# Loading w2 in fourteen parts instead of two in a transformer block on one core

## The chip, the cores and the metric

The kernel runs on one core of a Trainium2 chip. The metric is the time of one launch on the device in microseconds (us), less is better. The engines are called as in the profile: PE (TensorE; PEld is its weight loads), ACT (ScalarE), DVE (VectorE), POOL (GpSimd) and SP (SyncE, which here only asks for DMA transfers).

## The reference

One pre-norm transformer block over 2048 rows of width 1024, all in bf16: 32 attention heads of width 32, softmax over all 2048 keys, then an MLP of width 3584 with the tanh form of gelu.

```python
x = A_x                                             # [1, 2048, 1024]
h = x + A_ref(layernorm(x), A_wqkv, A_wo)           # attention with softmax, output projection
h2 = h + B_ref(layernorm(h), B_w1, B_b1, B_w2, B_b2)

def B_ref(x, w1, b1, w2, b2):                       # w1 [1024, 3584], w2 [3584, 1024]
    h = gelu(x @ w1 + b1)
    return h @ w2 + b2
```

## The kernel before

**Stages.** The rows are cut into four chunks of 512 (`CH`, numbers 0 to 3). At the start x is loaded, normalized and turned, and keys, values and the first queries are made. Then attention runs over chunk after chunk: for each chunk, head group and half of the chunk, steps of QK^T on PE (`qk`, L1132), exp on ACT (L1141, tiles `PT`), and the product with V and with ones on PE (`pv`, L1217). While chunk n is in attention, PE does the MLP of chunk n-1 in between; the output projection and the norms belong to that, and for chunks 0 and 1 the queries of chunk n+2. The last chunk's MLP comes after all attention, in `tail`.

**Who sets the order.** A planner written in Python (`Plan`) runs while the kernel is built. It keeps an estimate of when each engine is free and when each buffer is ready, and writes every instruction into the list of its engine in the order in which it decides on it. The generators (`ffn`, `rows_out`, `tail`) hand it MLP work in small pieces: at each `yield Need(...)` the planner may put attention work first. So the order on each engine is fixed when the kernel is built; on the chip each engine goes through its list, and semaphores hold it where an operand isn't there.

**SP's list.** All transfers of the kernel are asked for by SP, in the order in which the planner recorded them. A transfer waits, on SP, for the last readers of the memory that it overwrites, and for the transfer that used its lane before: weights go round through six lanes (`lanes_w`, L274), each with a semaphore of its own, so the seventh weight transfer waits until the first has landed. What stands behind a waiting transfer in SP's list waits too.

**The MLP of a chunk (`ffn`, L1425).** The up stage makes 28 groups (`fc`, 128 of the 3584 columns each): 8 matmuls of 512 rows with w1. w1 comes in 14 pieces of 512 KB in two buffers (`loader`, L1379): piece `bk + 1` is asked for at the second group of piece `bk`. PE's matmuls here are cut into four of 32 columns (`wide`, L529), so one of them stands as four in the profile. DVE adds the bias (L1494), then DVE and ACT make the gelu (L1506 to L1509, tanh on ACT), into `gT`.

The down stage takes w2 in four quarters of 256 output columns, `q` = 0 to 3. A quarter is 3584 x 256 values, 1792 KB, 28 blocks of 128 rows. For each quarter `rows_out` runs twice (`t` = 0 and 2), each time over two tiles of 128 rows with 28 blocks: 112 matmuls of 256 columns for a quarter, and 4 for the bias. DVE adds the residual (L1412) into `ost`, and a transfer stores 128 KB; behind every second quarter's store, in chunks 0 and 1, two loads of 128 KB fetch rows of x for the next chunk (`hch`).

**Where w2 lies and when it is asked for.** Quarters 0 and 2 lie at `w2_off`, quarters 1 and 3 at `hn_off`, where the turned rows `hnT` and part of w1's buffers were in the up stage. `load_w2` (L1389) asks for a quarter as two halves of 896 KB, each with one buffer mark, so PE's first matmul of a half waits for the whole half. Quarter 0 is asked for at group 22 of the up stage (L1490), quarter 1 after the up stage (L1516), quarters 2 and 3 when quarters 0 and 1 have been recorded (L1521), as their places come free then. In `tail` quarters 0 and 1 are asked for at its beginning, and 2 and 3 as in `ffn`, at other addresses.

Of the kernel before, what the change touches and what calls it, by code (L numbers as in the profile page):

```python
# [7 lines left out]
dt = mybir.dt  # L8
# [5 lines left out]
P = 128  # L14
# [221 lines left out]
def build_kernel(nc, A_x, A_wqkv, A_wo, B_w1, B_b1, B_w2, B_b2, out):  # L236
    _, S, D = A_x.shape
# [6 lines left out]
    FC = F // P  # L244
# [29 lines left out]
    lanes_w = lanes("dw", 6)  # L274
# [5 lines left out]
    def dma(out_ap, in_ap, nbytes, reads=(), writes=(), lanes=None, noncontig=False, is_out=False, eng=E.SP):  # L280
        flow, token = lanes.next()
        if is_out and flow not in out_flows:
            out_flows.append(flow)

        def fn(s):
            if noncontig:
                with nc.allow_non_contiguous_dma(reason="strided gather"):
                    return s.dma_start(out_ap, in_ap)
            return s.dma_start(out_ap, in_ap)

        plan.task(eng, fn, reads=reads, writes=list(writes) + [token], flow=flow, nbytes=nbytes)
# [29 lines left out]
    def sb(name, shape, dtype, bufs=None, at=None):  # L321
        nbytes = mybir.dt.size(dtype)
        for d_ in shape[1:]:
            nbytes *= d_
        off = cursor[0] if at is None else at
        h = nc.alloc_sbuf_tensor_at(name, shape, dtype, offset=off)
        if at is None:
            cursor[0] = off + (nbytes + 63) // 64 * 64
        if bufs is None:
            bufs = [Buf()]  # L330
        plan.track(off, off + nbytes, bufs)
        return h, bufs

    def nbufs(n):
        return [Buf() for _ in range(n)]
# [8 lines left out]
    biasm, _ = sb("biasm", [P, G, NCH], dt.float32)  # L344
# [35 lines left out]
    v_off = cursor[0]  # L380
# [25 lines left out]
    B_ps = nbufs(8)  # L406
# [851 lines left out]
    def ffn_alloc():  # L1258
        cursor[0] = region0
        f = ffn_bufs  # L1260

        def area(name, nbytes):
            f[name] = cursor[0]
            cursor[0] += nbytes

        area("g_off", FC * 1024)
        area("x3_off", 4 * 2048)
        area("hn_off", DC * 1024)
        f["w1_off"] = cursor[0]
        f["w1"], f["B_w1"] = sb("w1", [P, 2, DC, 256], dt.bfloat16, nbufs(2))  # L1270
        f["w2_off"] = cursor[0]
        f["w2"], f["B_w2"] = sb("w2", [P, 2, FC // 2, 256], dt.bfloat16, nbufs(2))
        f["NG"] = 3
        f["tm_off"] = cursor[0]
        f["tm"], f["B_tm"] = sb("tm", [P, 3, 2, 512], dt.bfloat16, nbufs(3))
        f["n12"] = [0, 0]
        assert cursor[0] <= nc.sbuf_usable_end, (cursor[0], nc.sbuf_usable_end)
# [108 lines left out]
                writes=[B_w1_[s]], lanes=lanes_w)  # L1386
        return load

    def load_w2(ci, q, at):  # L1389
        w2, B = sb(f"w2_{ci}_{q}", [P, 2, FC // 2, 256], dt.bfloat16, nbufs(2), at=at)  # L1390
        for h in range(2):
            dma(w2[:, h, :, :], B_w2[h * FC * 64:(h + 1) * FC * 64, q * 256:(q + 1) * 256].rearrange("(c p) d -> p c d", p=P), FC * P * 256,
                writes=[B[h]], lanes=lanes_w)
        return w2, B

    def rows_out(ci, q, t, w2_, gT, B_g, g_ch, ost, B_ost, hch, B_hch):
        w2, B_w2_ = w2_
        bank = fbanks.next()
        quad = tiled[0]
        for u in range(2):  # L1400
            lo = (t + u) * P
            for fc in range(FC):
                h, i = fc // (FC // 2), fc % (FC // 2)
                if fc % 2 == 0:
                    yield Need(B_g(fc) + B_g(fc + 1) + [B_w2_[h]], [B_ps[bank]] if u == 0 and fc == 0 else [],
                               [g_ch[fc + 1]] if fc + 1 in g_ch else [])
                wide(bank, u * 256, 256, gT[:, fc, lo:lo + P], w2[:, h, i, :], fc == 0, False,
                     B_g(fc) + [B_w2_[h]], [B_ps[bank]] if fc == 0 else [], False, quad)
            wide(bank, u * 256, 256, ident[:, q:q + 1].to_broadcast([P, P]), b2row[:], False, True,
                 [B_ident, B_b2row], [B_ps[bank]], True, quad)  # L1410
        o = (q * 2 + t // 2) % len(B_ost)
        dve(lambda v: v.tensor_tensor(ost[:, o, :, :], ps[:, bank, :].rearrange("p (u c) -> p u c", u=2),  # L1412
                                      hch[:, t:t + 2, q * 256:(q + 1) * 256], ALU.add),
            reads=[B_ps[bank]] + [B_hch[2 * (t + u) + q // 2] for u in range(2)], writes=[B_ost[o]], cost=690)
        r0 = CH[ci][0] + t * P

        def store():
            dma(out2[r0:r0 + 2 * P, q * 256:(q + 1) * 256].rearrange("(u p) c -> p u c", p=P), ost[:, o, :, :], 131072,
                reads=[B_ost[o]], lanes=lanes_o, is_out=True)
            if ci < NCH - 2 and q % 2:  # L1420
                for u in range(2):
                    load_rows(r0 + 512 + u * P, t + u, q // 2)
        stores.append(chain([("call", store, [B_ost[o]], [], 0)]))

    def ffn(ci):  # L1425
# [58 lines left out]
        for bk in range(FC // 2):  # L1484
            s = w1s[bk]
            for u in range(2):
                fc = bk * 2 + u
                if u == 1:
                    load_w1(bk + len(B_w1_) - 1)
                if fc == FC - 6:  # L1490
                    w2s = [load_w2(ci, 0, f["w2_off"])]

                def evac(bank, fc=fc):
                    dve(lambda v: v.tensor_scalar(gT[:, fc, 0:w], ps[:, bank, 0:w], b1f[:, fc:fc + 1], 0.5, ALU.add, ALU.mult),  # L1494
                        reads=[B_ps[bank], Bf_b1f], writes=[B_gT[fc]], cost=100 + 1.2 * w)
                    if fc % 2 == 0:
                        return
                    gs = gelu_i[0] % NG
                    gelu_i[0] += 1
                    for c_ in list(g_ch.values()):  # L1500
                        if c_.steps and c_.slot == gs:
                            flush(c_)
                    t_, x_ = tm[:, gs, :, :], gT[:, fc - 1:fc + 1, :]
                    Bt, Bx = B_tm_[gs], B_gT[fc - 1:fc + 1]
                    g_ch[fc] = chain([
                        (E.DVE, lambda v: v.tensor_tensor(t_, x_, x_, ALU.mult), Bx, [Bt], 690),  # L1506
                        (E.DVE, lambda v: v.scalar_tensor_tensor(t_, t_, GB, x_, ALU.add, ALU.mult), [Bt] + Bx, [Bt], 1220),  # L1507
                        (E.Activation, lambda a: a.activation(t_, t_, ACT.Tanh, scale=GK), [Bt], [Bt], 946),  # L1508
                        (E.DVE, lambda v: v.scalar_tensor_tensor(x_, t_, 1.0, x_, ALU.add, ALU.mult), [Bt] + Bx, Bx, 1220)])  # L1509
                    g_ch[fc].slot = gs  # L1510

                yield from group([(w1[:, s, dc, u * P:(u + 1) * P], hnT[:, dc, 0:w]) for dc in range(DC)], evac,
                                 lambda i, s=s: [B_w1_[s]] + B_hnT[:n4], n=w)
        no = 8 if ci < LAST - 1 else 4
        ost, B_ost = sb(f"ost{ci}", [P, no, 2, 256], dt.bfloat16, nbufs(no), at=x3_at)
        w2s.append(load_w2(ci, 1, f["hn_off"]))  # L1516
        for q in range(4):
            for t in range(0, n4, 2):
                yield from rows_out(ci, q, t, w2s[q], gT, lambda fc: [B_gT[fc]], g_ch, ost, B_ost, hch, B_hch)
            if q < 2:  # L1520
                w2s.append(load_w2(ci, q + 2, f["hn_off"] if q else f["w2_off"]))  # L1521
            if q == 1 and ci == LAST - 1:
                yield from last_norm(0)
        plan.track(f["w1_off"], f["w1_off"] + 8192, B_w1_)
# [5 lines left out]
    def tail():  # L1530
# [3 lines left out]
        load_w1 = loader(w1, B_w1_, [0], w1s)  # L1534
        for bk in range(6):
            load_w1(bk)
        w2s = [load_w2(LAST, q, v_off + q * 14336) for q in range(2)]
        yield from last_norm(1)
        nd = Need()
        nd.barrier = True  # L1540
# [7 lines left out]
        def part(bank, o, fc, hf, opens):  # L1548
            hn, B_hn = last["hn", hf]
            s = w1s[fc // 2]  # L1550
            for dc in range(DC):
                yield Need([B_w1_[s]] + B_hn, [B_ps[bank]] if opens and dc == 0 else [])
                wide(bank, o, 256, w1[:, s, dc, fc % 2 * P:fc % 2 * P + P], hn[:, dc, :], dc == 0, dc == DC - 1, [B_w1_[s]] + B_hn,
                     [B_ps[bank]] if dc in (0, DC - 1) else [], dc == DC - 1, False)
# [21 lines left out]
        for q in range(4):  # L1576
            for t in (0, 2):
                yield from rows_out(LAST, q, t, w2s[q], gT, lambda fc: [B_gT[2 * fc + t // 2]], {}, ost, B_ost, hch, B_hch)
            if q < 2:
                w2s.append(load_w2(LAST, q + 2, v_off + q * 14336))  # L1580

    def fill_total(ci):
        w = CH[ci][1]
# [206 lines left out]
```

## Time and profile before

| | us |
|---|---|
| three runs: median (lowest to highest) | 1184.12 (1182.95 to 1188.19) |
| the profiled execution | 1184.54 |
| its span on the core | 1182.7 |
| PE busy, of the span | 1105.1 |
| ACT busy | 1044.2 |
| DVE busy | 668.1 |

TensorE's granted clock was 0.992 in the mean. The profile also gives the span in 40 slices, where a digit is the busy share of an engine in tenths; the DMA queues with their packets; the chain of work that ended last; and, from the trace, a timeline of each engine, where a bracket says how long the engine stood idle before a row and what ended that. "Issue" there means that the profile shows nothing that the engine waited for.

The stages of chunk 0 as an example, from the timelines of PE and SP: its up stage runs from 374 to 466 us, its four quarters begin at about 466, 490, 516 and 541 us, each some 25 us with the attention work that lies in between.

| transfers, as the page lists them | KB each | median us from issue to landing |
|---|---|---|
| w2 halves, 32 | 896 | 8.0 |
| w1 pieces in `ffn`, 42 | 512 | 3.8 |
| stores of `ost`, 24 | 128 | 3.3 |
| rows of x for `hch`, 24 | 128 | 2.7 |

### The profile page before, as it was taken

What the parts mean: (1) busy time and instruction counts of PE and PEld (TensorE: products, weight loads), DVE (VectorE), ACT (ScalarE), POOL (GpSimd) and SP (SyncE); (2) the same over time, 40 slices, a digit from 0 to 9 for tenths busy, and PEclk for the clock granted to TensorE, in tenths of its full rate; (3) what the DMA queues carried; (4) which work ended last, traced back from release to release, by engine and by line L of the source; (5) the groups of instructions that cost most, each with busy time, mean ns of one, the idle gap of its engine ahead of it and who ended that gap; (6) DMA issues with size and microseconds to landing.
All of it is one profiled execution on the core that took longest, in us unless ns stands there. A gap on an engine that the chain in (4) does not pass through costs nothing.

```text
span 1182.7 us, 54817 instructions
## 1 busy us (share of the span) xinstructions
PE 1105.1 (93%) x25609; PEld 669.0 (57%) x25614; DVE 668.1 (56%) x1178; ACT 1044.2 (88%) x1155; POOL 21.2 (2%) x60
## 2 busy tenths in 40 slices
PE   6999999999998999999999999899999999999998
PEld 3646455554444444667444445667444456577887
DVE  8564555555655788344666877444668854543001
ACT  7798999899999999999999999989999999992400
POOL 2100000000000000000000000000000000000000
PEclk9999999999999999999999999999999999999999
DMA  8301000003401236230502253330033532208523
GB/s 232 81 21 39 21 3 12 12 9 95 100 12 56 74 89 164 76 97 22 149 12 75 75 151 84 88 83 22 19 108 91 140 84 75 70 17 225 154 78 85
DMA packets 177614, 91.62 MB, mean 77 GB/s; under 512 B 39653, under 2 KB 174825, under 8 KB 177385
## 3 DMA queue, kind: packets, MB, share of 16 engines
q1 hardware_dynamic: 177384, 88.10, 27.8%
q8 instruction: 200, 3.28, 1.1%
q14 instruction: 30, 0.24, 0.1%
HBM read 83.90 MB, written 4.19 MB: 74 GB/s over the span
## 4 chain that ended last, share of the span: by engine, by line
ACT 43%; PE 42%; issue 9%; DVE 6%; DMA 0%; POOL 0%; ACTq 0%; DVEq 0%; POOLq 0%
ACT PT L1141 39%; PE ps L529 18%; PE ps L524 9%; PE ps L1217 7%; PE ps L1132 6%; ACT tm L1508 3%; DVE lnst L481 1%; PE ps L803 1%; DVE Rg L1230 1%; DVE Rg L1228 1%; DVE QT L1232 1%; PE ps L858 1%; DVE gT L1494 0%; DVE rcp L1229 0%; DVE gT L1509 0%
## 5 line engine op out<-in xcount | busy, mean ns | idle before, releaser
L1141 ACT ACTIVATE PT<-ps 128x1024 bf16<-128x1024 f32 x1024 | 953.5, 1122 | 30.0 <-PE ps L1132 19.2
L1166 DVE TENSOR_TENSOR FS<-PT 128x1024 bf16<-128x1024 bf16 x245 | 167.7, 688 | 157.7 <-ACT PT L1141 111.7
L1217 PE MATMUL ps<-PT,V 128*32 128x256 bf16 x4096 | 226.2, 274 | 18.7 <-ACT PT L1141 10.6
L1132 PE MATMUL ps<-QT,KT 32*128 32x256 bf16 x4096 | 204.7, 274 | 20.6 <-ACT PT L1141 16.7
L529 PE MATMUL ps<-w,gT 128*32 128x256 bf16 x5376 | 178.3, 275 | 7.8 <-issue 7.1
L529 PE MATMUL ps<-hnT,w 128*32 128x512 bf16 x2688 | 173.0, 381 | 6.0 <-DVE gT L1494 4.0
L1132 PEld LDWEIGHTS ps<-QT,KT 32*128 32x128 bf16 x4096 | 60.9, 92 | 170.1 <-ACT PT L1141 152.1
L529 PEld LDWEIGHTS ps<-w,gT 128*32 128x32 bf16 x5376 | 142.0, 98 | 19.6 <-issue 13.0
L1217 PEld LDWEIGHTS ps<-PT,V 128*32 128x32 bf16 x4096 | 105.4, 96 | 74.2 <-ACT PT L1141 21.8
L1217 PE MATMUL ps<-PT,ones 128*32 128x256 bf16 x2136 | 136.9, 273 | 0.0
L529 PEld LDWEIGHTS ps<-hnT,w 128*32 128x32 bf16 x2688 | 61.8, 96 | 76.8 <-issue 28.0
L1494 DVE TENSOR_SCALAR gT<-ps,b1f 128x512 bf16<-128x512 f32 x84 | 63.0, 750 | 53.9 <-PE ps L529 52.9
L1217 PE MATMUL ps<-FS,ones 128*32 128x256 bf16 x980 | 70.4, 277 | 0.3 <-DVE FS L1166 0.2
L1217 PEld LDWEIGHTS ps<-PT,ones 128*32 128x32 bf16 x2136 | 57.3, 97 | 10.8
L529 PE MATMUL ps<-xnTe,wk 128*32 128x512 bf16 x832 | 57.9, 402 | 4.3 <-DVE kmax L646 2.3
L1545 ACT ACTIVATE gT_t<-ps,b1f 128x512 bf16<-128x512 f32 (+1 forms) x36 | 20.5, 591 | 42.4 <-PE ps L524 42.4
L1412 DVE TENSOR_TENSOR ost_t<-ps,hch_t 128x512 bf16<-128x512 f32 x8 | 5.5, 692 | 88.0 <-PE ps L524 88.0
L1509 DVE SCALAR_TENSOR_TENSOR gT<-tm,gT 128x1024 bf16<-128x1024 bf16 x42 | 51.2, 1219 | 3.5 <-ACT tm L1508 3.1
L1507 DVE SCALAR_TENSOR_TENSOR tm<-tm,gT 128x1024 bf16<-128x1024 bf16 x42 | 51.3, 1220 | 0.7
L524 PE MATMUL ps<-w,gT_t 128*128 128x256 bf16 x448 | 50.7, 273 | 0.0
L524 PE MATMUL ps<-hn_t,w_t 128*128 128x256 bf16 x448 | 49.2, 273 | 0.9 <-DVE hn_t L1350 0.9
L1508 ACT ACTIVATE tm<-tm 128x1024 bf16<-128x1024 bf16 x42 | 50.1, 1193 | 0.0
(139 smaller groups left out, 942.4 us busy)
## 6 DMA issues: line engine op xcount, KB each, us to landing
w<-in_B_w_dram SPq DMA_DIRECT2D x32, 896.0 KB, 8.0
w<-in_B_w_dram SPq DMA_DIRECT2D x42, 512.0 KB, 3.8
w_t<-in_B_w_dram SPq DMA_DIRECT2D x14, 512.0 KB, 7.0
xr<-in_A_x_dram SPq DMA_DIRECT2D x16, 256.0 KB, 6.8
wk<-in_A_wqkv_dram SPq DMA_DIRECT2D x16, 256.0 KB, 3.0
wq<-in_A_wqkv_dram SPq DMA_DIRECT2D x16, 256.0 KB, 5.1
hch<-in_A_x_dram SPq DMA_DIRECT2D x24, 128.0 KB, 2.7
out_dram<-ost SPq DMA_DIRECT2D x24, 128.0 KB, 3.3
```

Source lines behind the costliest of these rows:

```text
L481: steps.append((E.DVE, lambda v, c=c: v.bn_stats(lnst[:, s, i, c * 6:(c + 1) * 6], x_ap[:, c * 512:(c + 1) * 512]), [B_x], [B], 690))
L524: pe(lambda p: p.matmul(ps[:, bank, lo:lo + n], lhsT, rhs, start=start, stop=stop), reads=reads, writes=writes, inc=inc, cost=mm(n))
L529: pe(lambda p, r=r: p.matmul(ps[32 * r:32 * r + 32, bank, lo:lo + n], lhsT[:, 32 * r:32 * r + 32], rhs, start=start, stop=stop, tile_posit ...
L1132: pe(lambda p, k=k, kt=kt, r=r, b=b: p.matmul(ps[:, b, k * 256:(k + 1) * 256], KT[32 * r:32 * r + 32, g, kt * P:(kt + 1) * P], QT[32 * r:3 ...
L1141: act(lambda a, safe, i=i, b=b: a.activation(PT[:, o_, 2 * i:2 * i + 2, :], ps[:, b:b + 2, :], ACT.Exp, bias=0.0 if safe else biasm[:, g, ...
L1166: dve(lambda v: v.tensor_tensor(FS[:, f_, :, :], PT[:, o_, :, 0:256], PT[:, o_, :, 256:512], ALU.add), reads=B_PT[o_], writes=[B_FS[f_]], ...
L1217: pe(lambda p, d=d, r=r, lhsT=lhsT, rhs=rhs, n=n: p.matmul(ps[32 * r:32 * r + 32, OD, d * 256:(d + 1) * 256], lhsT, rhs, start=(start and ...
L1494: dve(lambda v: v.tensor_scalar(gT[:, fc, 0:w], ps[:, bank, 0:w], b1f[:, fc:fc + 1], 0.5, ALU.add, ALU.mult), reads=[B_ps[bank], Bf_b1f], ...
L1507: (E.DVE, lambda v: v.scalar_tensor_tensor(t_, t_, GB, x_, ALU.add, ALU.mult), [Bt] + Bx, [Bt], 1220),
L1508: (E.Activation, lambda a: a.activation(t_, t_, ACT.Tanh, scale=GK), [Bt], [Bt], 946),
L1509: (E.DVE, lambda v: v.scalar_tensor_tensor(x_, t_, 1.0, x_, ALU.add, ALU.mult), [Bt] + Bx, Bx, 1220)])
L1545: act(lambda a: a.activation(gT[:, fc, lo:lo + n], ps[:, bank, o:o + n], ACT.Gelu_apprx_tanh, bias=b1f[:, fc:fc + 1], scale=1.0), reads=[B ...
```

## The change

In chunks 0 to 2 a quarter of w2 is asked for in 14 parts of 128 KB (two blocks of 128 rows each), and each part has a buffer mark of its own, so that PE waits part by part. `load_w2` only makes the list of parts. In `ffn` the parts of quarter 0 are asked for one at a time from group 14 of the up stage on, one at each group; those of quarter q+1 at every eighth block of quarter q's `rows_out` (16 places, of which 14 are used). What is left when a quarter begins is asked for at once. The tail (`whole=True`) still takes two halves, with seven buffer marks each. Places in memory and the matmuls are as before.

```diff
-    def load_w2(ci, q, at):
-        w2, B = sb(f"w2_{ci}_{q}", [P, 2, FC // 2, 256], dt.bfloat16, nbufs(2), at=at)
-        for h in range(2):
-            dma(w2[:, h, :, :], B_w2[h * FC * 64:(h + 1) * FC * 64, q * 256:(q + 1) * 256].rearrange("(c p) d -> p c d", p=P), FC * P * 256,
-                writes=[B[h]], lanes=lanes_w)
-        return w2, B
+    def load_w2(ci, q, at, whole=False):
+        w2, B = sb(f"w2_{ci}_{q}", [P, FC, 256], dt.bfloat16, nbufs(FC // 2), at=at)
+        parts = deque()
+        n = FC // 2 if whole else 2
+        for c in range(0, FC, n):
+            def part(c=c):
+                dma(w2[:, c:c + n, :], B_w2[c * P:(c + n) * P, q * 256:(q + 1) * 256].rearrange("(c p) d -> p c d", p=P), n * P * 512,
+                    writes=B[c // 2:(c + n) // 2], lanes=lanes_w)
+            parts.append(part)
+        while whole and parts:
+            parts.popleft()()
+        return w2, B, parts
...
-    def rows_out(ci, q, t, w2_, gT, B_g, g_ch, ost, B_ost, hch, B_hch):
-        w2, B_w2_ = w2_
+    def rows_out(ci, q, t, w2_, gT, B_g, g_ch, ost, B_ost, hch, B_hch, coming=None):
+        w2, B_w2_, parts = w2_
+        while parts:
+            parts.popleft()()
...
             for fc in range(FC):
-                h, i = fc // (FC // 2), fc % (FC // 2)
+                if fc % 8 == 0 and coming:
+                    coming.popleft()()
                 if fc % 2 == 0:
-                    yield Need(B_g(fc) + B_g(fc + 1) + [B_w2_[h]], [B_ps[bank]] if u == 0 and fc == 0 else [],
+                    yield Need(B_g(fc) + B_g(fc + 1) + [B_w2_[fc // 2]], [B_ps[bank]] if u == 0 and fc == 0 else [],
...
-                if fc == FC - 6:
+                if fc == FC // 2:
                     w2s = [load_w2(ci, 0, f["w2_off"])]
+                if fc >= FC // 2:
+                    w2s[0][2].popleft()()
...
-        w2s.append(load_w2(ci, 1, f["hn_off"]))
         for q in range(4):
+            if q < 3:
+                w2s.append(load_w2(ci, q + 1, f["w2_off"] if q % 2 else f["hn_off"]))
             for t in range(0, n4, 2):
-                yield from rows_out(ci, q, t, w2s[q], gT, lambda fc: [B_gT[fc]], g_ch, ost, B_ost, hch, B_hch)
-            if q < 2:
-                w2s.append(load_w2(ci, q + 2, f["hn_off"] if q else f["w2_off"]))
+                yield from rows_out(ci, q, t, w2s[q], gT, lambda fc: [B_gT[fc]], g_ch, ost, B_ost, hch, B_hch, w2s[-1][2] if q < 3 else None)
...
-        w2s = [load_w2(LAST, q, v_off + q * 14336) for q in range(2)]
+        w2s = [load_w2(LAST, q, v_off + q * 14336, True) for q in range(2)]
...
-                w2s.append(load_w2(LAST, q + 2, v_off + q * 14336))
+                w2s.append(load_w2(LAST, q + 2, v_off + q * 14336, True))
```

More of the change, by code (lines that the diff above doesn't have):

```diff
@@ L1271, in ffn_alloc @@
         f["w2_off"] = cursor[0]
-        f["w2"], f["B_w2"] = sb("w2", [P, 2, FC // 2, 256], dt.bfloat16, nbufs(2))
+        f["w2"], f["B_w2"] = sb("w2", [P, FC, 256], dt.bfloat16, nbufs(2))
         f["NG"] = 3
@@ L1402, in rows_out @@
             for fc in range(FC):
-                h, i = fc // (FC // 2), fc % (FC // 2)
+                if fc % 8 == 0 and coming:
+                    coming.popleft()()
                 if fc % 2 == 0:
-                    yield Need(B_g(fc) + B_g(fc + 1) + [B_w2_[h]], [B_ps[bank]] if u == 0 and fc == 0 else [],
+                    yield Need(B_g(fc) + B_g(fc + 1) + [B_w2_[fc // 2]], [B_ps[bank]] if u == 0 and fc == 0 else [],
                                [g_ch[fc + 1]] if fc + 1 in g_ch else [])
-                wide(bank, u * 256, 256, gT[:, fc, lo:lo + P], w2[:, h, i, :], fc == 0, False,
-                     B_g(fc) + [B_w2_[h]], [B_ps[bank]] if fc == 0 else [], False, quad)
+                wide(bank, u * 256, 256, gT[:, fc, lo:lo + P], w2[:, fc, :], fc == 0, False,
+                     B_g(fc) + [B_w2_[fc // 2]], [B_ps[bank]] if fc == 0 else [], False, quad)
             wide(bank, u * 256, 256, ident[:, q:q + 1].to_broadcast([P, P]), b2row[:], False, True,
```

## The prediction

> **What bounds the kernel now.** I read the page first, then the waits of each engine, then TensorE's (PE) and ScalarE's (ACT) timelines in steps of 20 us, then the DMA queues in narrow windows.
>
> ```profile
> PE 1105.1 (93%) x25609; PEld 669.0 (57%) x25614; DVE 668.1 (56%) x1178; ACT 1044.2 (88%) x1155; POOL 21.2 (2%) x60
> ...
> PE   6999999999998999999999999899999999999998
> ...
> ACT  7798999899999999999999999989999999992400
> ...
> ACT 43%; PE 42%; issue 9%; DVE 6%; DMA 0%; POOL 0%; ACTq 0%; DVEq 0%; POOLq 0%
> ```
>
> The reader is to see two engines that are both nearly full, and no share for DMA in the chain that ended last. From about 230 to 1067 us ACT stands in one unbroken run of exponentials and tanh: its timeline shows idle time in only a dozen places there. So time that ACT loses there is lost for good, and PE's idle time counts only where it makes ACT idle. The tail (1070 to 1183, PE busy 108.6 of 113.0) is PE alone, and its length hangs on nothing that the change touches.
>
> The change moves loads of w2, so I looked at what happens while those loads run. In 491 to 498 us, during the third quarter's load of the first chunk, the queues show:
>
> ```profile
> q1 hardware_dynamic: 3727, 1.89, 94.0%
> ```
>
> and in the page as a whole there is a queue of another kind:
>
> ```profile
> q8 instruction: 200, 3.28, 1.1%
> ```
>
> 200 packets of 16,384 bytes are PE's program: PE has 25,609 + 25,614 instructions, and 200 x 256 = 51,200. In 485 to 491 us this queue has 2 packets, in 491 to 498 us it has none, in 498 to 502 us again 2. The timelines at that place and at its fellows (PE, then ACT; the bracket is the idle time before the row and what ended it):
>
> ```profile
> 500.44 1.05 PE L529 MATMUL ps<-w,gT 128*32 128x256 bf16 x30 [2.32 <-issue]
> ...
> 522.45 0.39 PE L529 MATMUL ps<-w,gT 128*32 128x256 bf16 x6 [0.93 <-issue]
> ...
> 759.37 0.84 PE L529 MATMUL ps<-w,gT 128*32 128x256 bf16 x24 [2.20 <-issue]
> ...
> 786.05 0.41 PE L1217 MATMUL ps<-PT,V 128*32 128x256 bf16 x4 [1.96 <-issue]
> ```
> ```profile
> 501.87 3.80 ACT L1141 ACTIVATE PT<-ps 128x1024 bf16<-128x1024 f32 x4 [2.31 <-PE ps L1132]
> ...
> 523.33 7.44 ACT L1141 ACTIVATE PT<-ps 128x1024 bf16<-128x1024 f32 x8 [0.97 <-PE ps L1132]
> ...
> 760.59 4.72 ACT L1141 ACTIVATE PT<-ps 128x1024 bf16<-128x1024 f32 x5 [2.20 <-PE ps L1132]
> ...
> 789.41 6.59 ACT L1141 ACTIVATE PT<-ps 128x1024 bf16<-128x1024 f32 x7 [3.01 <-PE ps L1132]
> ```
>
> PE stands still "for nothing that the profile shows", in the midst of a row of matmuls of one tile whose operands are all there. Eight such stops lie in 370 to 1070 us: before 500.44, 522.45, 706.79, 735.44, 759.37, 786.05, 994.33 and 1019.00, of 2.32 + 0.93 + 0.69 + 0.38 + 2.20 + 1.96 + 1.28 + 1.47 = 11.2 us. Counting PE's instructions, each restart falls on the same place, 189 instructions into a block of 256, and 1.3 to 1.4 us after the end of an instruction packet. All eight follow a w2 load (SP issued pairs of 896 KB at 489.99, 515.71, 725.55, 750.30, 776.64, 984.71, 1009.38, and one between w1's loads from 699.06 on). So PE runs out of program: the fetch of its next 16 KB stands behind w2's packets. An undisturbed fetch starts when PE is some 215 instructions into its block; these start 2.5 to 4.2 us later than that, 3.3 us in the mean. What PE has in hand covers 1.3 to 2.8 us of it (lateness less stop, stop by stop), and the rest is the stop. [...]
>
> **The change part by part.** In the built programs the order of instructions on PE, ACT, DVE and POOL is the same before and after; only SP's queue and the semaphores waited for differ.
>
> *The two 896 KB loads of a quarter become 14 of 128 KB* (chunks 0 to 2, 4 quarters each; the tail keeps halves). What it removes is the long queue in front of the fetch: 1.8 MB at once, about 8 us of traffic (7.4 and 8.6 us to landing in these windows). ACT's idle time at the eight stops is 2.31 + 0.97 + 0.83 + 0.35 + 2.20 + 3.01 + 1.26 + 1.44 = 12.4 us, and ACT is what bounds there, so 12.4 us is the most that these stops can give. PE can follow: in 466 to 570 us it is busy 97.3 of 104 us, and 3.3 of its idle time are two of the stops.
>
> What a fetch still waits for behind parts isn't in the trace, so it gets two bounds. The low one is nothing: fetches that start with a 128 KB store or a pair of 128 KB hch loads in the 4 us before them (as at 481.77 and 509.37) start at the usual 200 to 260 instructions. The high one: a part waits for the part six before it on its lane (lanes_w, L274), so at most 6 x 131 KB = 786 KB stand in the queue; at 275 GB/s, the mean of 491.3 to 498 us, that is 2.9 us, against 3.3 us now. With the stops' own cover this leaves 1.4 + 1.3 + 0.2 + 0.1 + 1.6 + 1.6 + 1.5 + 0.2 = 7.9 us. Between them: SP issues a load in 0.37 us (the shortest and the median of its rows), 354 GB/s, against 275 served; over the 9 parts that it can send in a row (below) that piles up 9 x 0.131 - 3.3 x 0.275 = 0.27 MB, 1.0 us of waiting, less than the least cover of 1.3 us. That is nearest to the low row. Some fetches in these stages have less in hand (0.4 us), so I keep 1.0 us of stops: gain 12.4 - 1.0 = 11.4 us.
>
> *SP's queue.* 12 quarters x 12 more issues x 0.37 us = 53 us, on an engine that waits some 500 us for PE on this kind of load alone. In the built order q+1's parts stand as nine, the store of the running quarter's first row pair, five; the five wait behind that store for DVE's ost. In the first chunk: quarter starts at 465.5, store issued at 479.0, five parts land by 479.0 + 5 x 0.4 + 3.3 (median landing of a 128 KB store) = 484, next quarter at 490.0. Stores and hch rows stand behind at most nine parts, 3.3 us; now the store at 517.02 already takes 3.40 us to issue behind a pair. Nothing on PE waits for either within a quarter. In the up stage each w1 load keeps its place ahead of the parts; the last three w2 parts go out right behind w1's last load, three groups of 92 / 28 = 3.3 us ahead of their quarter, some 10 us, against 3.8 us in which w1's 512 KB land and 3.3 us for a part.
>
> *PE's waits.* 138 more matmul rows wait, one for each part. In today's trace the step from one such group of four matmuls to the next is 109 ns in the median with a wait that is already met and without one: nothing. Six of them need a separate semaphore instruction, 51 ns each: 0.3 us, in PE's own slack. If a part were late, everything in PE's order behind it would stand, QK^T too, and then ACT.
>
> Sum: the profiled execution took 1184.54 us (span 1182.7, 1.8 around it); 1184.5 - 11.4 = 1173.1. The median of the runs shown lies 0.4 us under that execution, so 1172.7 us.
>
> **The rivals.**
> *Parts still hold the fetch.* If the fetch waits for all that is outstanding and six parts always are, 7.9 us of stops stay: 1184.1 - 12.4 + 7.9 = 1179.6. For it: while 256 KB loads follow each other in 566 to 577 us, the fetches at 572.85 and 577.67 start late (350 and 303 instructions in). Against: those pieces are twice as large, and SP can hardly keep six parts in flight at 0.37 us each.
> *The stops have another cause, or come back elsewhere.* Then no change, 1184. Against: eight of eight on one boundary, none without a load. For: ACT idles 0.84, 0.84 and 1.05 us in load windows at 473.71, 966.95 and 969.95 away from the boundary, from the fixed order of the work alone. [...]
> *Slower: the parts land in a row and too late.* A quarter has 4 row tiles x 28 steps of w2; the last part is used first after 26 of these 112 steps, 5.8 of 25 us. It has 25 + 5.8 = 30.8 us from the first request, 2.2 us a part. If each landed only after the one before, at the 2.7 us of the 128 KB hch rows, 14 take 37.8 us, 7.0 us too late, in 9 quarters 63 us: 1184.1 - 12.4 + 63 = 1235. Against: hch_t's four 256 KB loads are issued within 1.97 us and land in 3.2 us in the median, so loads overlap; with six in flight 14 parts take 14 x 2.7 / 6 = 6.3 us. [...]
>
> **How the numbers follow.** Forecast 0.70, parts still hold the fetch 0.17, no effect 0.07, late parts 0.06. A measurement of this kernel can tell about 0.5% from no change, 5.9 us: under 1178.2 is faster. Faster has the forecast and a third of the second case: 0.76. Same has the rest of it and most of the third: 0.17. Slower: 0.07. The range: low end 1169.0, if the three idle places away from the boundary go as well (12.4 + 2.7 = 15.1 us); high end 1180, the second case. Outside stand the third and fourth, 0.13, and a little of the others.
>
> **What would show it.** In the profile after: no PE idle time put down to "issue" of over 0.5 us in 370 to 1070; ACT's idle time for PE's QK^T down from 19.2 us to under 9; instruction packets every 3.6 to 4 us through the load windows; attention's end, at 1067 now, near 1056; no PE wait for a w2 load. The steps are wrong if the stops vanish and the time stays (ACT does not bound), if stops of over 1 us remain (the parts hold the fetch), or if PE waits for w2 at the head of a quarter.

## The result, and the profile after

| | before | after |
|---|---|---|
| median (lowest to highest), us | 1184.09 (1182.95 to 1188.19) | 1170.71 (1167.78 to 1173.69) |
| the profiled execution, us | 1184.54 | 1167.78 |
| its span, us | 1182.7 | 1166.0 |
| mean granted clock of TensorE | 0.992 | 0.999 |

The ratio of the times is 0.9881 with a 95% interval of 0.9845 to 0.9917: faster by 13.4 us in the medians, by 9.8 to 18.4 us at the ends of the interval. The times go with the granted clock of the run: the change's four took 1167.78, 1169.32, 1172.10 and 1173.69 us at 0.999, 0.997, 0.993 and 0.991. Before's runs beside the experiments took 1178.56 (one run), 1180.99, 1184.68 and 1185.96 us in the mean at these four clocks, so at the same clock the two kernels lie 10.8 to 12.6 us apart. The instructions of PE, ACT, DVE and POOL, and their order, are those of before.

The page of the kernel after, in the lines that answer to those shown of before (busy times, the 40 slices, the instruction queue, and the chain that ended last):

```profile
PE 1097.2 (94%) x25609; PEld 666.4 (57%) x25614; DVE 668.2 (57%) x1178; ACT 1042.3 (89%) x1155; POOL 21.1 (2%) x60
...
PE   6999999899998999999999999999989999999998
...
ACT  7798999899999999999999999999999999992400
...
q8 instruction: 200, 3.28, 1.2%
...
PE 43%; ACT 41%; issue 8%; DVE 7%; DMA 0%; POOL 0%; ACTq 0%; DVEq 0%; POOLq 0%
```

Busy times are nearly what they were; what went is idle time. The same 200 packets bring the same program. The 8 among the nines of the ACT row at slice 27 of 40 is gone.

Where PE waited in 370 to 1070 us, before and then after (us in total, times, longest):

```profile
PE ps L529 <- issue: 7.8, 6, 2.3
...
PE ps L1217 <- issue: 2.0, 1, 2.0
```
```profile
PE ps L529 <- issue: 0.8, 1, 0.8
...
PE ps L506 <- issue: 0.3, 1, 0.3
```

With L1132's one wait of 1.5 us before, and L524's of 0.2 after, PE's time at "issue" went from 11.3 to 1.3 us. No row of this view names a DMA of w2 as the releaser: no part was late. Before had no such row either, so it isn't the marks by which PE now waits part by part that gain. ACT's waits for QK^T over the whole span (19.2 us, 15 times, before) are now:

```profile
ACT PT L1141 <- PE ps L1132: 4.5, 6, 1.1
```

The timeline of ACT after, at the places of the first two, the fourth, the fifth and sixth, and the last two of the eight stops: the rows of exponentials have no break there, and no bracket. (At the third, too, the timeline has no bracket.)

```profile
489.49 52.41 ACT L1141 ACTIVATE PT<-ps 128x1024 bf16<-128x1024 f32 x57
...
722.55 1.17 ACT L1519 ACTIVATE tm<-tm 128x1024 bf16<-128x1024 bf16 x1
723.50 16.72 ACT L1141 ACTIVATE PT<-ps 128x1024 bf16<-128x1024 f32 x18
...
744.56 56.19 ACT L1141 ACTIVATE PT<-ps 128x1024 bf16<-128x1024 f32 x61
...
989.47 58.88 ACT L1141 ACTIVATE PT<-ps 128x1024 bf16<-128x1024 f32 x64
```

In a window of 675 us ACT's busy time shows the same (after the stretch and its length: busy us and count of PE, PEld, DVE, ACT, POOL, then granted clock, DMA share, GB/s), before and then after:

```profile
370.00:1045.00 675.00, 635.76 (x16336) 368.01 (x16328) 424.45 (x667) 659.38 (x717) 6.69 (x15) 0.99 0.30 82
```
```profile
370.00:1045.00 675.00, 645.78 (x16800) 377.82 (x16796) 431.94 (x680) 672.16 (x732) 6.66 (x15) 1.00 0.29 82
```

**Where the 16.7 us between the two spans went.** I set the two timelines of ACT side by side, instruction by instruction. Up to about 216 us, before the first load of w2, after is 2.65 us ahead: the change does nothing there, and the clock differs (last section). At the places of the eight stops it gains 2.45, 1.33, 0.85, 0.56, 2.35, 3.34, 1.40 and 1.85 us, 14.1 in all. It gains some 1.5 us at 967 to 970 us, again a place where the clock differs. It loses 0.71 and 0.40 us, 1.1 in all, at two small stops that are new:

```profile
569.80 0.61 PE L529 MATMUL ps<-wo(1, 0)_97,QT 128*32 128x512 bf16 x8 [0.81 <-issue]
...
851.83 0.29 PE L506 MATMUL ps<-ident,x 128*32 128x128 bf16 x7 [0.31 <-issue]
```

2.65 + 14.1 + 1.5 - 1.1 = 17.2; the 0.5 over the 16.7 is spread in small losses. The two new stops stand, as the old ones did, 189 instructions into a block of 256, the first beside the 1 MB loads of wo. Without the two clock places the profiled pair differs by about 12.6 us. Of the 3.34 us at the sixth stop some 1 us is likely the clock's too: PE stood 1.96 us there and ACT 3.01, while at the other seven stops the two differ by 0.14 us at most, and a stretch of half clock follows that stop (last section). Attention ends at 1049.9 instead of 1066.9 us.

SP's queue at the first chunk's second quarter after, as its timeline has it (start, duration, line, transfer, count):

```profile
489.25 5.23 SPq L289 DMA_DIRECT2D w<-in_B_w_dram  x8
499.23 0.38 SPq L289 DMA_DIRECT2D out_dram<-ost  x1
...
502.09 8.73 SPq L289 DMA_DIRECT2D w<-in_B_w_dram  x6
```

For quarters 1 to 3 "one at a time" is so in the program's text only: SP takes most of a quarter's parts in a row, here eight in 5.23 us, 0.65 us a part.

### The profile page after: what moved, and what is told of

It is laid out like the page before. It is cut to its first block, busy times and chain, and to the rows that moved or that the text cites. A ratio compares the mean times of both kernels' runs of the same rounds, so it can differ in the third digit from the quotient of the medians.

```text
span 1166.0 us, 54971 instructions
## 1 busy us (share of the span) xinstructions
PE 1097.2 (94%) x25609; PEld 666.4 (57%) x25614; DVE 668.2 (57%) x1178; ACT 1042.3 (89%) x1155; POOL 21.1 (2%) x60
## 3 DMA queue, kind: packets, MB, share of 16 engines
HBM read 83.90 MB, written 4.19 MB: 76 GB/s over the span
## 4 chain that ended last, share of the span: by engine, by line
PE 43%; ACT 41%; issue 8%; DVE 7%; DMA 0%; POOL 0%; ACTq 0%; DVEq 0%; POOLq 0%
ACT PT L1141 38%; PE ps L529 18%; PE ps L524 9%; PE ps L1217 8%; PE ps L1132 6%; ACT tm L1519 2%; PE ps L803 1%; DVE Rg L1230 1%; DVE QT L1232 1%; DVE Rg L1228 1%; DVE lnst L481 1%; DVE gT L1505 1%; PE ps L858 1%; DVE rcp L1229 0%; DVE gT L1520 0%
## 5 line engine op out<-in xcount | busy, mean ns | idle before, releaser
L1217 PE MATMUL ps<-PT,V 128*32 128x256 bf16 x4096 | 225.9, 274 | 17.5 <-ACT PT L1141 11.1
L1132 PE MATMUL ps<-QT,KT 32*128 32x256 bf16 x4096 | 203.6, 273 | 19.3 <-ACT PT L1141 16.6
L529 PE MATMUL ps<-w,gT 128*32 128x256 bf16 x5376 | 174.6, 273 | 0.7 <-DVE gT L1505 0.4
L1132 PEld LDWEIGHTS ps<-QT,KT 32*128 32x128 bf16 x4096 | 60.7, 92 | 167.9 <-ACT PT L1141 155.5
L524 PE MATMUL ps<-w,gT_t 128*128 128x256 bf16 x448 | 50.7, 273 | 0.0
L524 PE MATMUL ps<-hn_t,w_t 128*128 128x256 bf16 x448 | 49.2, 273 | 0.9 <-DVE hn_t L1350 0.9
```

The costliest lines, as they stand in the source:

```text
L524: pe(lambda p: p.matmul(ps[:, bank, lo:lo + n], lhsT, rhs, start=start, stop=stop), reads=reads, writes=writes, inc=inc, cost=mm(n))
L529: pe(lambda p, r=r: p.matmul(ps[32 * r:32 * r + 32, bank, lo:lo + n], lhsT[:, 32 * r:32 * r + 32], rhs, start=start, stop=stop, tile_posit ...
L1132: pe(lambda p, k=k, kt=kt, r=r, b=b: p.matmul(ps[:, b, k * 256:(k + 1) * 256], KT[32 * r:32 * r + 32, g, kt * P:(kt + 1) * P], QT[32 * r:3 ...
L1217: pe(lambda p, d=d, r=r, lhsT=lhsT, rhs=rhs, n=n: p.matmul(ps[32 * r:32 * r + 32, OD, d * 256:(d + 1) * 256], lhsT, rhs, start=(start and ...
```

## The experiments

All of them compute with the order of PE's, ACT's and DVE's instructions that before and after share, so times differ by waits alone, but for what x7 leaves out. Diffs are against the change, x10's against before. The question left was not whether the stops come from the fetch of PE's program, but what such a fetch waits for: all that is outstanding when it is due (the queue), the whole of the transfer that is being moved, or a turn that is bounded; and whether the small size of the transfers, their spacing or the earlier start does the work.

Two quantities are worked out from the records for every fetch in the quarters' stages. *Lateness* is the start of the fetch's packet less the time at which PE passes instruction 215 of its block. *Outstanding* is what SP had asked for less what the queues had begun to move, at that time; it is given in KB of 1000 bytes, the sizes of transfers in KB of 1024.

| kernel | median (lowest to highest), us | ratio to before, with interval | stage, us | PE at "issue", us | lateness, mean / most, us |
|---|---|---|---|---|---|
| the change | 1170.71 (1167.78 to 1173.69) | 0.9881 (0.9845 to 0.9917) | 836.7 | 1.3 | 0.34 / 0.76 |
| x11_change_again | 1172.39 (1170.63 to 1172.52) | 0.9893 (0.9863 to 0.9923) | 839.1 | 1.4 | 0.52 / 1.01 |
| x1_at_once | 1174.68 (1174.17 to 1175.49) | 0.9916 (0.9887 to 0.9945) | 841.5 | 0.4 | 0.68 / 1.73 |
| x2_448k_spread | 1175.64 (1172.32 to 1176.56) | 0.9923 (0.9897 to 0.9949) | 843.7 | 5.2 | 1.82 / 2.93 |
| x3_256k_at_once | 1171.23 (1171.0 to 1174.43) | 0.9896 (0.9864 to 0.9929) | 840.6 | 2.4 | 1.07 / 1.79 |
| x4_half_1lane | 1182.09 (1178.14 to 1185.99) | 0.9977 (0.996 to 0.9993) | 852.5 | 8.6 | 1.89 / 3.36 |
| x5_one_1792k | 1183.54 (1181.2 to 1188.31) | 1.0006 (0.9979 to 1.0033) | 851.0 | 11.1 | 2.70 / 4.02 |
| x6_256k_7lanes | 1170.94 (1168.38 to 1173.08) | 0.9896 (0.984 to 0.9952) | 839.4 | 0.4 | 1.35 / 2.89 |
| x7_one_part | 1168.36 (1167.54 to 1172.0) | 0.9883 (0.9827 to 0.9939) | 837.3 | 0.3 | |
| x8_wo_wq_parts | 1168.96 (1165.66 to 1170.95) | 0.9885 (0.983 to 0.9939) | 836.5 | 0.6 | 0.51 / 0.97 |
| x9_q0_spread | 1168.87 (1166.0 to 1172.3) | 0.9872 (0.9839 to 0.9906) | 837.2 | 0.5 | 0.59 / 1.40 |
| x10_q0_early | 1182.99 (1179.91 to 1189.11) | 0.9988 (0.9966 to 1.001) | 854.3 | 9.5 | 2.59 / 4.55 |

The stage is that of the profiled execution from ACT's 214th instruction (at 212 to 216 us) to the end of attention; it is 851.0 us before. It leaves out what differs before w2's first load, but not the clock (last section). PE's "issue" is in 370 to 1070 us, 11.3 us before. Lateness here is over the fetches that had more than 180 KB outstanding ahead of them (12 to 20 for each kernel; before: 2.50 / 4.19). Each ratio is to runs of before beside which the kernel ran.

### Size or spacing: x1_at_once and x3_256k_at_once

x1 keeps the 128 KB parts and asks for all 14 at once, at the places where before asked for its halves. x3 is x1 with parts of 256 KB.

```diff
-                if fc == FC // 2:
+                if fc == FC - 6:
                     w2s = [load_w2(ci, 0, f["w2_off"])]
...
-        while whole and parts:
+        while parts:
             parts.popleft()()
```
```diff
-        n = FC // 2 if whole else 2
+        n = FC // 2 if whole else 4
```

> Quarters in 14 parts of 128 KB as after the change, but all 14 asked for at once, at the places where the two halves were asked for before (group 22, end of the up stage, end of the quarter before). Theory 'queue' (a fetch of PE's program waits for the w2 traffic that is outstanding, which six lanes and SP's 0.37 us a part keep short): no stops put down to issue over 0.5 us in the quarters, 1170 to 1174. Rival 'spacing' (it is the asking one at a time during the steps that helps): the eight stops of 11 us are back, 1183 to 1185. Rival 'grain' (a fetch gets its turn between two transfers, so the size of one transfer decides): 1170 to 1174.

> Seven parts of 256 KB, all asked for at once at the old places, six lanes: up to 1.5 MB outstanding, as SP issues 256 KB in 0.37 us. Queue: stops of 6 to 11 us, 1178 to 1184. Grain: one part is 0.95 us, less than PE has in hand: no stops, 1170 to 1173. Spacing: 1183 to 1185.

x1 has no stop beside w2 either, with all parts asked for together: the small parts do it, not their spacing. Whether they do it by their size, or by the little that is outstanding with them (some 0.4 MB at most when a fetch was due), x1 can't tell; x3 and x6 can. But it has a wait of a new kind, seen in PE's waits and in its timeline:

```profile
PE ps L529 <- DMA w<-in_B_w_dram: 4.8, 4, 1.9
```
```profile
456.06 1.91 PE L529 MATMUL ps<-hnT,w 128*32 128x512 bf16 x32 [1.61 <-DMA w<-in_B_w_dram]
```

These are matmuls of the up stage (`hnT`), and what is late is w1. SP's timeline shows why:

```profile
440.47 13.41 SPq L289 DMA_DIRECT2D w<-in_B_w_dram  x17
```

The 14 parts of quarter 0 stand in SP's list between two pieces of w1, and w1's next piece is asked for after them. So the spacing is worth something at quarter 0 only (here the 4.8 us), and not for the fetch. x1's median of 1174.68 us lies just above the 1170 to 1174 that were expected, where this wait was not thought of. In time x1 and the change aren't clearly apart (their intervals overlap), though at the same granted clock, 0.993, x1 took 1174.17 and 1174.90 us and the change with its repeat 1172.10 to 1172.52; the 4.8 us are shown by the trace.

x3's parts of 256 KB leave 2.4 us of stops, in small pieces of at most 0.8, where the size of the transfer alone was to leave none and the queue 6 to 11 us. It is as fast as the change within the intervals.

### Middle-sized transfers, and large ones one at a time: x2_448k_spread and x4_half_1lane

x2 asks at the places of the change for parts of 448 KB. x4 goes back to the halves of 896 KB, at the old places, but puts w2's loads on one lane of their own, so that the second half is asked for only when the first has landed. It has the change's 14 marks a quarter, but seven are set together when a half has landed.

```diff
-        n = FC // 2 if whole else 2
+        n = FC // 2 if whole else 7
```
```diff
+    lanes_2 = lanes("dz", 1)
...
-        n = FC // 2 if whole else 2
+        n = FC // 2 if whole else 14
...
-                    writes=B[c // 2:(c + n) // 2], lanes=lanes_w)
+                    writes=B[c // 2:(c + n) // 2], lanes=lanes_w if whole else lanes_2)
```

> The change's places, but four parts of 448 KB a quarter in place of 14 of 128 KB. Queue: nothing ties SP to PE's steps, so all four go out in about 1.5 us, 1.8 MB stand in the queue as before: stops of 8 to 12 us, 1180 to 1185. Spacing: asked for in four steps, so about 1171. Grain: one part is 448 KB / 275 GB/s = 1.7 us, hardly over what PE has in hand (1.3 to 2.8 us): stops under 2 us in all, 1171 to 1173.

> Two halves of 896 KB at the old places as before the change, but on one lane of their own, so that the second is asked for when the first has landed: at most 0.9 MB outstanding. The marks are part by part. Queue: a fetch waits for what is left of one half, up to 3.3 us, on average half of it; stops of 3 to 7 us, 1175 to 1180. Grain: the single transfer is as large as before, so stops of 9 to 12 us, 1181 to 1185. Spacing: 1183 to 1185.

x4 has at most 997 KB outstanding, against 1688 before, and still stops for 8.6 us: between what the queue was to give (3 to 7) and what the size of the transfer was to give (9 to 12), and nearer to the second. Of its fetches with over 690 KB ahead of them six waited 2.2 to 3.4 us, until 84 KB in the mean were left. Its PE also waits 3.5 us for w1, since SP is held by the lane. So to limit what is outstanding, with transfers that stay at 896 KB, hardly brings a gain: the ratio is 0.9977.

x2 limits nothing: 0.96 MB were outstanding in the mean, against 1.04 before. It stops for 5.2 us, and its median is 1175.64 us; none of the three expectations had that (8 to 12 us of stops for the queue, under 2 for the size, 1171 us for the spacing). So transfers of 448 KB bring part of the gain, with as much outstanding as before.

### Much outstanding, in small transfers, and in one large one: x6_256k_7lanes and x5_one_1792k

x6 is x3 with seven lanes for w2 alone, so that SP may ask for a whole quarter without a wait. x5 asks for a quarter in one transfer of 1792 KB at the old places.

```diff
+    lanes_2 = lanes("dz", 7)
...
-        n = FC // 2 if whole else 2
+        n = FC // 2 if whole else 4
```
```diff
-        n = FC // 2 if whole else 2
+        n = FC // 2 if whole else 28
```

> Seven parts of 256 KB at once at the old places, on seven lanes of their own, so that no part waits for another and all 1.8 MB stand in the queue within some 2.6 us. Queue (outstanding bytes decide): as before the change, lateness up to 4 us, stops of 9 to 12 us, 1181 to 1185. Theory 'transfer size decides': as with six lanes shared: lateness under 1.9 us, stops of 1 to 2 us, 1170 to 1174.

> A quarter as one transfer of 1792 KB, at the old places. So far the lateness of a fetch went with the size of the transfer: about 1.4 us at 128 KB, 1.7 at 256, 2.5 at 448, 2.2 to 4.2 at 896. Theory 'whole transfer' (a fetch waits until the transfer in progress is done on its DMA engine): lateness of 4 to 7 us, stops of 25 to 40 us in all, 1198 to 1215. Rival 'bounded turn' (an engine takes a bounded number of packets of one queue before it serves the other, and 896 KB are already past that): lateness 2.5 to 4.2 us and stops of 9 to 13 us as before the change, 1182 to 1186.

x6's DMA view in 484 to 496 us (packets, MB, share of 16 engines), and SP's row there:

```profile
q1 hardware_dynamic: 3422, 1.71, 53.9%
q8 instruction: 2, 0.03, 1.3%
```
```profile
488.26 4.58 SPq L290 DMA_DIRECT2D w<-in_B_w_dram  x7
```

SP asks for the whole quarter within 4.58 us, not the 2.6 that were expected, so never all of it is outstanding: up to 1038 KB stand ahead of a fetch. PE has no stop over 0.2 us in 370 to 1070, though one fetch was 2.89 us late, where under 1.9 was expected. With one transfer a quarter all stops of before are back. That allows a comparison at the same amount outstanding. Fetches in the quarters with 690 to 1050 KB ahead of them (three fetches that got in before the load's first packets are left out):

| size of one transfer | kernels | fetches | outstanding when due, mean | lateness, mean (range), us | outstanding at the fetch, mean |
|---|---|---|---|---|
| 1792 KB | x5 | 3 | 906 KB | 3.07 (2.82 to 3.24) | 108 KB |
| 896 KB | before, x10, x4 | 12 | 890 KB | 2.90 (2.17 to 3.78) | 113 KB |
| 448 KB | x2 | 3 | 997 KB | 2.38 (1.78 to 2.80) | 423 KB |
| 256 KB | x3, x6 | 18 | 831 KB | 1.43 (0.75 to 2.89) | 803 KB |

The last column counts also what SP asked for only after the fetch was due. Of the bytes that stood ahead of it when it was due, some 0.43 of 0.83 MB were still to come behind transfers of 256 KB, 0.27 of 1.00 behind 448 KB, and 0.05 of 0.9 at most behind the two larger sizes. So here, in transfers of 896 KB and more, the fetch waited until nearly everything ahead of it was gone, and in transfers of 256 KB it passed about half of it. The queue as the only cause falls by that. In before itself the fetch with the most ahead of it, 1688 KB in two halves, started after 2.43 us with 0.94 MB left, as much as the whole second half.

The whole transfer as the rule falls by x5: a fetch that was due with 1764 KB ahead of it, nearly all of one transfer, started after 3.31 us with some 730 KB of them left, and no fetch of x5 was later than 4.02 us, though a transfer of 1792 KB took 9.5 us from issue to landing in the median, and one of 128 KB, in the change, 3.5. What is left is a wait that grew with the size of the transfers (1.43 us in the mean at 256 KB, 2.38 at 448, 2.90 at 896, 3.07 at 1792) and was never over 4.6 us in these runs. x5's times are those expected of the bounded turn (2.70 us of lateness in the mean, 11.1 us of stops, 1183.54 us), but no run shows a bound itself, and how the DMA engines come to this wait isn't settled. The records don't say on which of the 16 DMA engines a packet ran, so it also isn't excluded that the fetch waits for a part of the engines only, whose share of the bytes was done earlier.

### The floor: x7_one_part

In chunks 0 to 2 only the first 128 KB of a quarter are loaded, and all 28 blocks of the quarter are multiplied with these two. So 13 of 14 parts of w2's traffic are left out, 20.5 of the 53.2 MB that the queues move in 370 to 1045 us.

```diff
+        parts = deque()
+        if not whole:
+            w2, B = sb(f"w2_{ci}_{q}", [P, 2, 256], dt.bfloat16, nbufs(1), at=at)
+            dma(w2[:], B_w2[0:2 * P, q * 256:(q + 1) * 256].rearrange("(c p) d -> p c d", p=P), 2 * P * 512, writes=B, lanes=lanes_w)
+            return w2, B * (FC // 2), parts
...
-                wide(bank, u * 256, 256, gT[:, fc, lo:lo + P], w2[:, fc, :], fc == 0, False,
+                wide(bank, u * 256, 256, gT[:, fc, lo:lo + P], w2[:, fc if ci == LAST else fc % 2, :], fc == 0, False,
```

> The floor: in chunks 0 to 2 only the first 128 KB of each quarter of w2 are loaded, at the old places, and every block of the quarter is multiplied with these two blocks, so that 26 of 28 blocks of w2 take no part in the result. PE's, ACT's and DVE's work is the same in kind and order. If w2's loads are the whole cause of the stops and the change's parts leave nothing of them, the time is that of the change within noise, 1168 to 1173, and no stop stands in the quarters; if parts still cost something, it is faster than the change by more than 3 us.

The stage takes 837.3 us without the traffic and 836.7 with it: in these two executions the parts cost nothing that can be seen. By the medians (1168.36, against 1170.71 and 1172.39) some 2 to 4 us could be left, but the intervals of the ratios overlap, and at the same granted clock, 0.993, x7 took 1172.00 us and the change with its repeat 1172.10 to 1172.52. So nothing more than the change gets is shown to be there for w2.

### The same cure elsewhere: x8_wo_wq_parts

The change, and besides it a half of wo in eight transfers of 128 KB instead of one of 1 MB, and the late pieces of wq in two of 128 KB, each with its own mark.

```diff
-        dma(h[:], A_wo[:, j * 512:(j + 1) * 512].rearrange("(g p) d -> p g d", p=P), 1 << 20, writes=B, lanes=lanes_w)
+        for g in range(G):
+            dma(h[:, g, :], A_wo[g * P:(g + 1) * P, j * 512:(j + 1) * 512], 1 << 17, writes=[B[g]], lanes=lanes_w)
```

> The change, and also wo's halves (1 MB) in 8 parts of 128 KB and the late wq pieces (256 KB) in two of 128 KB, with a mark for each. In the profile after the change one stop of 0.81 us stands at 569.80 beside these loads (fetch 3.6 us late). Theory 'transfer size decides': the fetches there are under 1.6 us late and the stop is gone, ACT's 0.48 us with it; the time is that of the change less 0.5 us, which no timing here can tell: 1168 to 1173. Rival (that stop has to do with the switch to the projection, not with the loads): it stays.

The stop at the loads of wo and wq, 0.81 us at 569.80 in the change, is gone; x8 cuts both, so it doesn't tell which of them held the fetch. It varies (0.3 us in x11, 0.5 in x9, none in x1 and x7), so the lateness of the fetch beside these loads says more: it is 3.6 us late in the change, 2.6 to 3.3 in x1, x7, x9 and x11, and under 1.2 in x8. The stop at the transposes, whose loads (four of 256 KB and w1's of 512 KB) x8 leaves alone, stays (in x11 it is 1.1 us):

```profile
PE ps L506 <- issue: 0.6, 1, 0.6
```

The time can't be told from the change's: the stage is 836.5 us against 836.7, and the intervals overlap.

### Which quarter needs the spacing, and the early start alone: x9_q0_spread, x10_q0_early, x11_change_again

x9 spreads the parts of quarter 0 as the change does and asks for quarters 1 to 3 all at once at the places of before. x10 is before, with its halves of 896 KB, but asks for quarter 0 at group 14. x11 is the change once more, beside these two.

```diff
-        while whole and parts:
+        while (whole or q) and parts:
```
```diff
-                if fc == FC - 6:
+                if fc == FC // 2:
```

> 128 KB parts; quarter 0 asked for one at a time from group 14 on, as in the change, but quarters 1 to 3 all at once at the places of before. In x1_at_once, where quarter 0 too was asked for at once, PE waited 1.6 and 1.9 us for w1, whose pieces stood behind the 14 parts in SP's list, and ACT lost some 3 us by that. If this is all that the asking one at a time gives: the time of the change within noise, 1168 to 1173, no PE wait for w1 and no stop over 0.5 us in the quarters. If spreading the later quarters matters too: 1174 and more, with stops there.

> The kernel before, with quarter 0's two halves asked for at group 14 in place of group 22 and nothing else. Theory: no more than the stop of 0.7 us at 706.79 moves or goes; stops of 9 to 12 us in the later quarters stay, 1182 to 1186. Rival (the earlier start of the down stage's loads is what gains): 1176 or less.

> The changed kernel once more, beside the two others on one chip, as the measure for x9_q0_spread: 1168 to 1174, no stop over 0.5 us in the quarters, a fetch there at most 1.0 us late.

x9 is as fast as the change: for quarters 1 to 3 the spacing did nothing that shows (1168.87 us, against 1170.71 and 1172.39). x10 is as slow as before, and PE's waits show the same stops:

```profile
PE ps L529 <- issue: 7.0, 5, 2.2
...
PE ps L1217 <- issue: 2.0, 1, 2.0
```

So the early start alone did nothing either (0.9988 of before). x9's median is 3.5 us under x11's and 1.8 under the change's; with intervals of 0.9839 to 0.9906 and 0.9863 to 0.9923 none of the variants is shown to beat the change.

## Why the prediction was right, and where it was off

*What bounds, and what the stops are.* Right. PE's "issue" went from 11.3 to 1.3 us, ACT's busy time in 675 us rose by 12.8 (672.16 - 659.38), and the time fell by 13.4. What PE lost at the stops, ACT had lost too. Large transfers brought the stops back (x5, 11.1 us at "issue"), small ones removed them however they were spread (x1 and x6, 0.4 us each), and without the traffic there were none at w2 (x7, 0.3 us).

*What a fetch waits for behind parts.* The lower end was right: a wait of 1.0 us was forecast, and 0.34 in the mean, 0.76 at most, were measured. The sum behind it was right by luck. It had 0.27 MB pile up because SP would ask for a part every 0.37 us, 354 GB/s, against 275 served. In the change a part takes 0.47 us of SP in the median, and eight in a row took 5.23 us, 200 GB/s, which is less than was served: by that sum nothing would pile up. All the same 0.28 MB in the mean (0.35 at most) were outstanding when a fetch was due, asked for and not yet begun; what held them wasn't traced. The step that failed is the upper bound: "at most 6 x 131 KB = 786 KB stand in the queue; at 275 GB/s [...] that is 2.9 us" takes it that a fetch waits for all that is outstanding. For transfers of 896 KB that came near (2.90 us at 890 KB). In transfers of 256 KB 831 KB cost 1.43 us, with about half of it still to come. The size of the single transfer counted here, not only the sum; the second case, with 7.9 us of stops and 1179.6 us, rested on the same step, and fell.

*The size of the gain.* Forecast 11.4 us, measured 13.4 by the medians, 11.2 by those of x11, and 10.8 to 12.6 at the same granted clock; so a part of the 13.4 is likely the clock's. "12.4 us is the most that these stops can give" was too low in the trace: ACT gains 14.1 us at the eight places. The sum had left out that ACT's rows overlap. In the change the rows at these eight places begin 0.12 to 0.31 us before the end of the one ahead of them, as the row above that begins at 723.50, before 722.55 + 1.17 = 723.72. A stop loses that besides its idle time, 1.75 us over the eight places, and 12.4 + 1.75 is the 14.1. Some 1 us of the 14.1 is likely the clock's, as said above. The 1.0 us kept for stops that stay came out by luck: there are none at w2, and 1.1 us at the two new places, beside wo and at the transposes, for which nothing was forecast. Attention ended 5.6 us before the forecast (1066.9 - 11.4 = 1055.5): some 1.7 from this term and 4.1 from the clock (2.65 + 1.5), less 0.2 of small differences.

*SP's queue and PE's waits.* Right: PE waits for no part of w2 in the change. That the parts of quarter 0 don't hold up w1 had been argued from the places in SP's list; x1 shows what it costs when they do (4.8 us of PE).

*The signs.* ACT's wait for QK^T fell to 4.5 us (forecast: under 9). The instruction packets that begin in 470 to 560 us come 3.3 to 6.0 us after the one ahead, 4.1 in the median, where before had gaps of up to 8.1; forecast were 3.6 to 4. "No stop over 0.5 us" was missed by one, the 0.81 us beside wo; cutting the loads of wo and wq in x8 took the lateness behind it away.

*The other rivals.* No effect is excluded by the interval, parts too late by PE's waits. The three idle places away from the boundary, put down to "the fixed order of the work alone", were of two kinds: ACT's 0.84 us at 473.71 and at 966.95 stand in the change as before (0.84 us at 471.08 and 954.53), and the 1.05 us at 969.95 are gone with the half clock there.

## What to carry to other kernels

Where PE runs a long unrolled program, look for idle time at "issue" that falls on one place of a block of 256 instructions while large transfers are under way: here the fetch of the program stood behind them (2.50 us late in the mean with 896 KB), and smaller single transfers let it through (128 KB: 0.34 to 0.68 us late; 256 KB: 1.07 and 1.35; 448 KB, in part: 1.82); one large transfer at a time (8.6 us of stops left of 11.3) or an earlier start (9.5 left) didn't. Then look at what the many small transfers stand in front of in the queue that asks for them: spread them where an urgent load comes behind, as w1 did here at quarter 0 (4.8 us of PE).

## What was not expected of the hardware

In these runs a fetch behind large transfers was late by 4.6 us at most, whether 0.9 or 1.8 MB stood ahead of it, and behind transfers of 256 KB by about half as much at the same amount (1.43 us against 2.90).

TensorE's granted clock was 0.50 in stretches that the clock records of before and of the change give as 3.413 us each. Apart from the last microseconds of the span there are five in before's profiled execution (at 117, 151, 213, 786 and 967 us; 0.992 in the mean), one in the change's (116; 0.999), five in x11's (0.993) and none in x8's (1.000). One such stretch in before (columns as in the window above):

```profile
786.00:789.40 3.40, 3.35 (x60) 2.02 (x64) 2.12 (x5) 0.39 (x1) 0.00 (x0) 0.50 0.03 10
```

PE was busy nearly all the time, with 60 matmuls at clock 0.50, just after the stop of 1.96 us that ended at 786.05. So part of ACT's 3.01 us of idle time there is likely the clock's. With four such stretches fewer the change's profiled execution lies at the low end of its runs, and the profiled pair differs by 16.8 us where the medians differ by 13.4.

In before each of the five begins within 0.8 us of PE's restart from an idle time of 1.06 to 2.37 us. Other idle times as long, such as the 2.32 us before 500.44, are followed by none. What sets a stretch off stays open.
